# One decode block on one core: heads 28 to 30 selected in two steps, the last head's last two value blocks as matmul weights, and a new order of the last three heads

## The chip, the cores and the metric

The kernel runs on one core of a Trainium2 chip, in float32 throughout. The metric is the device time of one execution in microseconds (us); of several executions the median is taken. "At 358.03" means 358.03 us after the start of the profiled span.

## What is computed

For a batch of 4 with one new token each, a block computes attention over a cache and then a small token-mixing network, both under an adaptive layer norm. Cut to what matters here:

```
q = (h @ wq) as 32 heads of 128;  k, v: 8 cached heads of 4096 x 128 per batch, each serving 4 query heads
p = softmax(q k^T / sqrt(128));   o = p v;   A = o @ wo
x = x + ga * A
h = layernorm(x) * (1 + cb) + sb;   u = gelu(h * w1 + b1) (1792 wide);   y = u . w2 + b2
x = x + gb * y
```

One pair of batch and cached head is called a head below; there are 32 of them, 0 to 31, and heads 24 to 31 belong to the last batch. Each reads 2048 KB of keys and as much of values: 134 of the 157 MB that the kernel loads.

## The kernel before

**Layout.** The scores of a head stand in PSUM as 128 partitions by 1024 columns: four groups of 32 partitions, each a quarter of the keys, made by four matmuls that write to four different groups (`scores`, L238). In each group only 4 of the 32 rows are query heads (a row every 8); the rest are padding. VectorE takes the maximum over a row (L243) and over the groups (L252), ScalarE the exponential with the row sums (L268, tile `p` and `l`), and VectorE transposes `p` in blocks of 32 (`turn`, L275, two halves), so that keys stand on partitions.

**Values of heads 0 to 30** (`values`, L301): 8 matmuls, each with 32 columns of `p` as weights and 512 columns of values moving. A product of 512 columns holds four key blocks of 128 side by side, and of the 128 partitions by 512 columns of the sum `pv` only those places count where a row's key block is that of the column. VectorE copies `pv` to `po` (`copy_v`, L315). The **selection** (`pick`, L324) is 4 matmuls with a 128 x 128 piece of `po` as weights and 4 columns of `sel` moving, summed into `pt` (128 x 4): `sel` holds a 1 at the rows that belong to a query head, times the reciprocal of the sum of exponentials (`sums`, L279; `scale`, L284 and L290). VectorE copies `pt` to `oT` (L329), and `project` multiplies it with `wo` (4 matmuls of 512 columns, L337; VectorE adds the result to `acc`, L353). A float32 matmul is two matmul instructions in the profile, each with a weight load: 4 matmuls appear as x8.

**Head 31** ends in another way (`values_last`, L309): 32 blocks of 128 keys, each one matmul with 32 columns of `p` as weights and 128 columns of values moving; four blocks run in four partition groups. So its sum `pve` is 128 x 128 and its selection one matmul. Heads 30 and 31 project (L342, 16 matmuls of 128 columns each) straight into one PSUM tile, `pgx`, to which a matmul with the identity (L685) adds `ep`, the residual with all earlier heads of the batch (fold L358, then L362 and L363 on VectorE). On `pgx` the layer norm begins (L370), and behind it the whole mixing network of the last batch.

**The order of the work.** From head 24 on it is written out by hand in a string, `PLAN`: each word is a step, its letter an operation, its number the head (and after the dot the part). Those spoken of here: `t` turn, `l` sums, `L` scale, `v` values, `V` copy_v, `a` pick, `A` copy_o, `p` project, `P` add_up, `x` and `g` a piece of the mixing network of batch 2 (VectorE L431, ScalarE L487), `f` a VectorE product of `wo` with a gate (L567), `y` the fold, `E` the residual, `I` the identity matmul, `LV` and `LW` loads. Each engine executes its own share strictly in this order.

**Loads.** All run on one queue, SP's, into a ring of three slots of 4 MB; a load waits only until its slot is free. The values of heads 30 and 31 arrive in pieces, cut at the blocks of `cuts`: (0, 16, 32) and (0, 16, 24, 28, 32). The last load, `LW`, is 1 MB of modulation weights.

**Buffers.** The pool `wk` gives two buffers to a tag unless another number is written; the small PSUM tiles (`pl`, `pm`, `pb`, `pt`, `pa`, `pc`, `pst`) share two buffers of the pool `ps_m`.

Of the kernel before, what the change touches and what calls it, by code (L numbers as in the profile page):

```python
# [8 lines left out]
F32 = mybir.dt.float32  # L9
I32 = mybir.dt.int32  # L10
AF = mybir.ActivationFunctionType
# [22 lines left out]
def adaln_decode(ctx: ExitStack, tc: tile.TileContext, small, x, wmod, wq, kk, kv, vv, wo, out):  # L34
# [53 lines left out]
    first = g32[:, 0:1].to_broadcast([P, 32])  # L88
    QT = cst.tile([P, B, HKV, 32], F32, name="QT")
# [187 lines left out]
    def sums(i):  # L277
        pl = ps_m.tile([P, 1], F32, name="pl", tag="m")
        mm(pl, grp if i < NS - 1 else grpl, PL[i][1], start=True, stop=True)  # L279
        SEL[i] = pl  # L280

    def scale(i):
        rl = wk.tile([P, 1], F32, name="rl")
        dv.reciprocal(rl, SEL[i])  # L284
        if i == NS - 1:
            SEL[i] = wk.tile([P, 1, REP], F32, name="sel", bufs=4)
            dv.tensor_scalar(SEL[i][:, 0], eight, rl, None, op0=OP.mult)
            return
        sel = wk.tile([P, 4, REP], F32, name="sel", bufs=4)
        dv.tensor_scalar(sel, sel4, rl, None, op0=OP.mult)  # L290
        SEL[i] = sel

    PV, PA = {}, {}

# [9 lines left out]
    def values_last(i, ks, pv):  # L304
        PV[i] = pv
        pT = PL[i][0].rearrange("p (k r) -> p k r", r=32)
        for k in ks:
            for c in range(4):
                mm(pv[32 * c:32 * c + 32, :], pT[:, k * 4 + c, :], VT[i][:, k * 4 + c, :],  # L309
                   start=(k == 0), stop=(k == 7))  # L310
# [7 lines left out]

    def pick(i):
        po, sel = PV.pop(i), SEL.pop(i)  # L320
        OT[i] = pt = ps_m.tile([P, REP], F32, name="pt", tag="m")
        n = po.shape[-1] // DH
        for c in range(n):
            mm(pt, po[:, c * DH:(c + 1) * DH], sel[:, c, :], start=(c == 0), stop=(c == n - 1))  # L324

    def copy_o(i):
        pt = OT[i]
        OT[i] = wk.tile([P, REP], F32, name="oT")
        dv.tensor_copy(OT[i], pt)  # L329

    def project(i, pa=None):
        b, h = divmod(i, HKV)
        oT = OT.pop(i)
        if pa is None:
            pa = ps_m.tile([P, D], F32, name="pa", tag="m")
            for g in range(REP):
                mm(pa[32 * g:32 * g + 32, :], oT[:, g:g + 1].to_broadcast([P, 32]), wo_t[h][:, g, :],  # L337
                   start=True, stop=True)
        else:
            for g in range(REP):  # L340
                for c in range(4):
                    mm(pa[32 * c:32 * c + 32, :], oT[:, g:g + 1].to_broadcast([P, 32]),  # L342
                       wo_t[h][:, g, c * P:(c + 1) * P], start=(g == 0 and h == HKV - 2),
                       stop=(g == REP - 1 and h == HKV - 1))
        PA[i] = pa
# [232 lines left out]
    for i in range(NS - HKV):  # L578
# [38 lines left out]
        if i == NS - HKV - 2:  # L617
# [7 lines left out]
    cuts = {NS - 1: (0, 16, 24, 28, 32), NS - 2: (0, 16, 32)}  # L625
    last = [(0, 1, 2, 3), (4, 5), (6,), (7,)]
# [6 lines left out]
    v28.1 b31 l30 B31 e31 LV31 V28 L30 c t30.1 a28 l31 L31 v29.0 t31.1 v29.1 A28 p28 t30.0 V29 a29 v30.0  # L633
    A29 LW f v30.1 P28 p29 g V30 t31.0 a30 x v31.0 v31.1 v31.2 P29 A30 Y y f v31.3 p30 E V31 a31 I A31 p31
# [3 lines left out]
             "l": sums, "L": scale, "V": copy_v, "a": pick, "A": copy_o, "P": add_up,  # L638
# [5 lines left out]
    for step in PLAN.split():  # L644
# [8 lines left out]
        elif op == "v":  # L653
            if i < NS - 1:
                values(i, range(4 * q, 4 * q + 4))
                continue
            if q == 0:
                pve = ps_s.tile([P, 8, P], F32, name="pve", tag="s")[:, 0]
            values_last(i, last[q], pve)
        elif op == "p":  # L660
            project(i, pgx[:, 4] if i >= NS - 2 else None)
# [19 lines left out]
        elif op == "E":  # L681
            ep = cst.tile([P, P], F32, name="ep")
            residual(ep, pc)
        elif op == "I":
# [50 lines left out]
```

## Time and profile before

| what | value |
|---|---|
| time, median of 3 runs | 389.92 us (388.86, 389.92, 390.04) |
| profiled execution: span from first to last instruction | 386.9 us |
| profiled execution: its own time | not listed apart from the three runs, which are 1.9 to 3.1 us above the span |
| TensorE busy, weight loads | 298.9 us, 122.4 us |
| VectorE, ScalarE busy | 215.2 us, 108.0 us |
| loaded from HBM | 157.32 MB, 407 GB/s over the span |
| mean granted TensorE clock | 0.877 of full speed |

In the profile PE is TensorE's matmuls, PEld its weight loads, DVE VectorE, ACT ScalarE and SPq the queue of SyncE, which issues the loads. A row of the timeline has start, duration, engine, line, operation, tiles and shapes; the brackets at its end tell how long the engine had been idle and what released it. The chain of waits is followed back from the last instruction, and its rows are start, duration and what ran or was waited for.

### The profile page before, as it was taken

To read this page: it belongs to the slowest core of one execution; us is meant where nothing else is said; L and a number is where in the kernel's file an instruction comes from. 1 tells how busy PE (TensorE), PEld (TensorE's weight loads), DVE (VectorE), ACT (ScalarE), POOL (GpSimd) and SP (SyncE) were. 2 spreads that over 40 slices of the span, in tenths; PEclk is the share of its full clock that TensorE was granted. 3 is DMA by queue.
4 is the path that set the end of the run, shared out by engine and by line. 5 is a ranking of instruction groups with operands and counts; after the bars stand their busy time and mean duration, and the time that the engine had idled before them with its cause. 6 is when DMAs were issued, how large, how long until landed. Compare 5 with 4: busy or idle time off the path is not lost.

```text
span 386.9 us, 5714 instructions
## 1 busy us (share of the span) xinstructions
PE 298.9 (77%) x2416; PEld 122.4 (32%) x2416; DVE 215.2 (56%) x516; ACT 108.0 (28%) x132; POOL 0.7 (0%) x6
## 2 busy tenths in 40 slices
PE   0765575863966949979888859999988887999984
PEld 0111121231323313334222323443323342444562
DVE  0420351620542524676766644676875579788766
ACT  0101120110110110113567210213783104757356
POOL 0000000000000000000000000000000000000000
PEclk9998875986695775989999985978999998899999
DMA  8999999999999999999999999999999999999910
GB/s 329 430 434 434 415 451 430 410 449 432 418 447 434 430 434 432 434 432 434 426 434 429 434 429 434 434 432 434 425 434 432 434 429 434 422 427 423 404 46 3
DMA packets 7281, 157.70 MB, mean 408 GB/s; under 512 B 964, under 2 KB 980, under 8 KB 1368
## 3 DMA queue, kind: packets, MB, share of 16 engines
q1 hardware_dynamic: 7248, 157.33, 94.8%
q8 instruction: 19, 0.31, 0.3%
q14 instruction: 6, 0.05, 0.0%
q10 hardware_dynamic: 8, 0.00, 0.0%
HBM read 157.32 MB, written 0.01 MB: 407 GB/s over the span
## 4 chain that ended last, share of the span: by engine, by line
DMA 54%; PE 28%; DVE 16%; issue 1%; SPq 1%; ACTq 0%; DVEq 0%
DMA kv<-in_kv 47%; PE s L238 8%; PE pv L301 7%; DMA wq<-in_wq 6%; DVE m L243 3%; DVE p L275 3%; PE pt L324 2%; PE pa L337 2%; PE pb L258 2%; DVE uu L431 1%; DVE mx L252 1%; DVE acc L353 1%; PE qs L152 1%; PE phb L417 1%; PE pve L309 1%
## 5 line engine op out<-in xcount | busy, mean ns | idle before, releaser
L238 PE MATMUL s<-kv,QT 128*32 128x512 f32 x512 | 76.2, 715 | 35.6 <-DMA kv<-in_kv 32.6
L268 ACT ACTIVATE p<-s,nm 128x1024 f32<-128x1024 f32 x32 | 35.6, 1114 | 199.0 <-DVE nm L263 198.9
L243 DVE TENSOR_REDUCE m<-s 128x1 f32<-128x1024 f32 x32 | 39.2, 1224 | 76.1 <-PE s L238 76.0
L301 PE MATMUL pv<-kv,p 128*32 128x512 f32 x496 | 75.0, 684 | 0.4 <-DMA kv<-in_kv 0.4
L275 DVE STREAM_TRANSPOSE p<-p 128x512 f32<-128x512 f32 x64 | 41.9, 687 | 1.7 <-ACT p L268 1.7
L324 PEld LDWEIGHTS pt<-sel,po 128*128 128x128 f32 x250 | 33.6, 208 | 28.7 <-issue 15.6
L238 PEld LDWEIGHTS s<-kv,QT 128*32 128x32 f32 x512 | 16.3, 125 | 81.3 <-DMA kv<-in_kv 45.3
L337 PE MATMUL pa<-wo,oT 128*32 128x512 f32 x240 | 35.3, 663 | 4.3 <-DVE oT L329 4.2
L324 PE MATMUL pt<-sel,po 128*128 128x4 f32 x250 | 36.2, 268 | 1.4 <-DVE po L315 1.4
L315 DVE COPY po<-pv 128x512 f32<-128x512 f32 x31 | 21.4, 689 | 17.0 <-PE pv L301 17.0
L252 DVE TENSOR_REDUCE mx<-pm 1x128 f32<-1x512 f32 x32 | 21.4, 671 | 0.8 <-PE pm L247 0.7
L258 PEld LDWEIGHTS pb<-neg,mx 1*128 1x128 f32 x64 | 10.8, 210 | 32.9 <-DVE mx L252 31.1
L487 ACT ACTIVATE u<-u 128x1024 f32<-128x1024 f32 x20 | 20.4, 1052 | 2.7 <-DVE u L431 2.6
L431 DVE TENSOR_SCALAR u<-hb,wr,sm 128x512 f32<-128x512 f32 x40 | 19.9, 541 | 1.0 <-PE py L442 0.9
L353 DVE TENSOR_TENSOR acc<-acc,pa 128x512 f32<-128x512 f32 x26 | 17.7, 681 | 3.6 <-PE pa L337 3.6
L268 ACT ACT_TABLE_LOAD x11 | 14.1, 1283 | 19.0 <-DVE nm L263 18.9
L137 PE MATMUL s<-wm,sT 128*4 128x512 f32 x16 | 8.4, 684 | 12.2 <-DVE sT L123 12.2
L258 PE MATMUL pb<-neg,mx 1*128 1x1 f32 x64 | 13.5, 278 | 5.3 <-DVE mx L252 5.3
L487 ACT ACT_TABLE_LOAD x13 | 16.7, 1283 | 0.2
L247 PE MATMUL pm<-ident,m 128*1 128x128 f32 x32 | 9.1, 286 | 9.8 <-DVE rl L284 3.8
L301 PEld LDWEIGHTS pv<-kv,p 128*32 128x32 f32 x496 | 14.1, 146 | 8.1 <-issue 2.1
L247 PEld LDWEIGHTS pm<-ident,m 128*1 128x1 f32 x32 | 2.5, 80 | 39.1 <-DVE rl L284 21.0
(144 smaller groups left out, 212.3 us busy)
## 6 DMA issues: line engine op xcount, KB each, us to landing
kv<-in_kv SPq DMA_DIRECT2D x28, 4096.0 KB, 20.8
wq<-in_wq SPq DMA_DIRECT2D x2, 4096.0 KB
wo<-in_wo SPq DMA_DIRECT2D x4, 2048.0 KB
kv<-in_kv SPq DMA_DIRECT2D x4, 2048.0 KB, 18.5
wm<-in_wmod SPq DMA_DIRECT2D x2, 2048.0 KB
kv<-in_kk SPq DMA_DIRECT2D x1, 4096.0 KB
kv<-in_vv SPq DMA_DIRECT2D x3, 1024.0 KB
wm<-in_wmod SPq DMA_DIRECT2D x1, 1024.0 KB
```

The costliest lines, as they stand in the source:

```text
L238: mm(s[32 * c:32 * c + 32, n * 512:(n + 1) * 512], QT[:, b, h, :], KT[i][:, (n * 4 + c) * 512:(n * 4 + c + 1) * 512], start=True, stop=True)
L243: dv.tensor_reduce(M[i], S[i], axis=AX.X, op=OP.max)
L252: dv.tensor_reduce(mx, M[i].rearrange("o (c r) -> o r c", c=4).unsqueeze(1).to_broadcast([1, 4, 32, 4]), axis=AX.X, op=OP.max)
L258: mm(pb, M[i].rearrange("o c r -> o (c r)"), neg1, start=True, stop=True)
L268: nc.scalar.activation(p, S[i], AF.Exp, bias=M.pop(i), accum_out=l)
L275: dv.transpose(p, p)
L301: mm(PV[i][32 * q:32 * q + 32, :], pT[:, 128 * k:128 * k + 128:4], VT[i][:, 4 * k:4 * k + 4, :].rearrange("p j d -> p (j d)"), start=(k < ...
L324: mm(pt, po[:, c * DH:(c + 1) * DH], sel[:, c, :], start=(c == 0), stop=(c == n - 1))
L337: mm(pa[32 * g:32 * g + 32, :], oT[:, g:g + 1].to_broadcast([P, 32]), wo_t[h][:, g, :], start=True, stop=True)
L353: dv.tensor_add(ACC[b], ACC[b], pa)
L431: dv.tensor_scalar(u[:, e, :], hb, wr[:, j:j + 1], b1[:, j:j + 1], op0=OP.mult, op1=OP.add)
L487: nc.scalar.activation(u, u, AF.Gelu_apprx_tanh)
```

## The change

Four things change.

1. **Heads 28, 29 and 30 select in two steps.** `scale` now spreads the reciprocals over 32 columns per key block (`sel32`, 128 x 128 in place of 128 x 16; 28 of 32 columns in a group are zero, from a constant `gsel` built at the start). `gather_heads` multiplies with these as weights and `po` moving: 4 matmuls of 128 columns into four partition groups of a PSUM tile `qo`. `copy_heads` copies `qo` to SBUF, on VectorE for head 28 and on ScalarE for 29 and 30. `pick` is then one matmul, with that copy as weights and 4 columns of a constant moving.
2. **The last head's last two blocks.** `values_last` does blocks 0 to 29. Blocks 30 and 31 (`values_end`) take the values themselves as weights (128 x 128) and 4 columns of `p` moving, straight into `pt`, and the selection of the other 30 blocks is added to the same tile. The scale by the reciprocal moves behind it: `sums` of head 31 makes four sums on all partitions (`le`, `pl4`), `scale` is a reciprocal of 4 columns, and `copy_o` of head 31 multiplies instead of copying.
3. **The cuts of head 31's values** become (0, 16, 24, 30, 32).
4. **A new order of the last lines of `PLAN`,** with head 30's projection in two halves.

```diff
+    gsel = cst.tile([P, 4, 32], F32, name="gsel")
+    dv.memset(gsel, 0.0)
+    dv.tensor_copy(gsel[:, :, 0:REP], sel4)
...
     def sums(i):
+        if i == NS - 1:
+            le = wk.tile([P, REP], F32, name="le", bufs=1)
+            dv.tensor_scalar(le, eight, PL[i][1], None, op0=OP.mult)
+            SEL[i] = ps_m.tile([P, REP], F32, name="pl4", tag="m")
+            mm(SEL[i], ones, le, start=True, stop=True)
+            return
...
     def scale(i):
+        if i == NS - 1:
+            rl4 = wk.tile([P, REP], F32, name="rl4", bufs=1)
+            dv.reciprocal(rl4, SEL[i])
+            SEL[i] = rl4
+            return
         rl = wk.tile([P, 1], F32, name="rl")
         dv.reciprocal(rl, SEL[i])
...
+        src, m = (gsel, 32) if i in TWO else (sel4, REP)
+        sel = wk.tile([P, 4, m], F32, name=f"sel{m}", bufs=4) if m == REP else wk.tile([P, 4, m], F32, name="sel32", tag="h1")
+        dv.tensor_scalar(sel, src, rl, None, op0=OP.mult)
...
+    TWO = (NS - 4, NS - 3, NS - 2)
+    ENDING = 30
...
+    def values_end(i):
+        pT = PL[i][0].rearrange("p (k r) -> p k r", r=32)
+        for j in range(ENDING, 32):
+            mm(OT[i], VT[i][:, j, :], pT[:, j, 0:32:8], start=(j == ENDING), stop=False)
...
+    def gather_heads(i):
+        po, sel = PV.pop(i), SEL.pop(i)
+        QO[i] = q = ps_m.tile([P, P], F32, name="qo", tag="m")
+        for c in range(4):
+            mm(q[32 * c:32 * c + 32, :], sel[:, c, :], po[:, c * DH:(c + 1) * DH], start=True, stop=True)
...
+        QO[i] = wk.tile([P, P], F32, name="qs", tag="a")
+        if i < NS - 3:
+            dv.tensor_copy(QO[i], q)
+        else:
+            nc.scalar.activation(QO[i], q, AF.Copy)
...
     def pick(i):
+        if i in TWO:
+            OT[i] = pt = ps_m.tile([P, REP], F32, name="pt", tag="m")
+            mm(pt, QO.pop(i), g32[:, 0:REP], start=True, stop=True)
+            return
+        if i == NS - 1:
+            mm(OT[i], PV.pop(i), eight, start=False, stop=True)
+            return
...
-        dv.tensor_copy(OT[i], pt)
+        if i == NS - 1:
+            dv.tensor_mul(OT[i], pt, SEL.pop(i))
+        else:
+            dv.tensor_copy(OT[i], pt)
...
-    cuts = {NS - 1: (0, 16, 24, 28, 32), NS - 2: (0, 16, 32)}
-    last = [(0, 1, 2, 3), (4, 5), (6,), (7,)]
+    cuts = {NS - 1: (0, 16, 24, ENDING, 32), NS - 2: (0, 16, 32)}
+    last = [range(8), range(8, 16), range(16, 24), range(24, ENDING)]
...
-    v28.1 b31 l30 B31 e31 LV31 V28 L30 c t30.1 a28 l31 L31 v29.0 t31.1 v29.1 A28 p28 t30.0 V29 a29 v30.0
-    A29 LW f v30.1 P28 p29 g V30 t31.0 a30 x v31.0 v31.1 v31.2 P29 A30 Y y f v31.3 p30 E V31 a31 I A31 p31
+    v28.1 b31 l30 B31 e31 LV31 V28 L30 c j28 J28 t30.1 a28 A28 l31 L31 v29.0 t31.1 v29.1 p28 t30.0 V29 P28
+    j29 J29 v30.0 a29 A29 LW t31.0 f v30.1 p29 g V30 P29 j30 J30 v31.0 a30 v31.1 f A30 Y x y v31.2 v31.3
+    p30.0 E V31 O v31.4 a31 p30.1 I A31 p31
```

Three places show how the change moves instructions. The numbers behind the tiles' names only tell buffers apart; `po_2333` and `po_2336` are head 28's in the two kernels.

TensorE where head 28 is selected and head 31's sums are made, before:

```order
L436 MATMUL py_2065<-u_2135,sm_88 32x128 x8
L324 MATMUL pt_2348<-sel_2255,po_2333 128x4 x4
L279 MATMUL pl_2353<-l_2327,grpl_118 128x1
L301 MATMUL pv_2359<-kv_2210,p_2235 32x512 x8
L337 MATMUL pa_2371<-wo4_126,oT_2369 32x512 x4
```

and in the changed kernel:

```order
L481 MATMUL py_2068<-u_2138,sm_88 32x128 x8
L341 MATMUL qo_2350<-po_2336,sel32_2258 32x128 x4
L357 MATMUL pt_2358<-g32_114,qs_2355 128x4
L285 MATMUL pl4_2364<-le_2362,ones_107 128x4
L313 MATMUL pv_2368<-kv_2213,p_2238 32x512 x8
L382 MATMUL pa_2378<-wo4_129,oT_2360 32x512 x4
```

Between the first and the second step of the selection there is now a copy by VectorE (`qs_2355`), and the sums of head 31 read `le_2362`, which VectorE makes, where before they read `l_2327` from ScalarE. Head 29's values stand behind both.

VectorE at the same place, before:

```order
L315 COPY po_2333<-pv_2295 128x512
L284 RECIPROCAL rl_2335<-pl_2322 128x1
L290 TENSOR_SCALAR sel_2337<-g32_114,rl_2335 128x16
L275 STREAM_TRANSPOSE p_2306<-p_2306 128x512
L284 RECIPROCAL rl_2355<-pl_2353 128x1
L287 TENSOR_SCALAR sel_2357<-g32_114,rl_2355 128x4
L275 STREAM_TRANSPOSE p_2326<-p_2326 128x512
```

and in the changed kernel:

```order
L331 COPY po_2336<-pv_2298 128x512
L297 RECIPROCAL rl_2338<-pl_2325 128x1
L300 TENSOR_SCALAR sel32_2340<-gsel_120,rl_2338 128x128
L347 COPY qs_2355<-qo_2350 128x128
L278 STREAM_TRANSPOSE p_2309<-p_2309 128x512
L374 COPY oT_2360<-pt_2358 128x4
L283 TENSOR_SCALAR le_2362<-g32_114,l_2330 128x4
L293 RECIPROCAL rl4_2366<-pl4_2364 128x4
```

`le_2362` stands behind the copy, a transpose of half of head 30's `p`, and `oT`. The third row, head 30's selection, takes the buffer of head 28's (`sel32_2258`: tag `h1` has two), so it waits until TensorE's four matmuls on `qo_2350` have read that.

TensorE from the values of head 31 to the layer norm, before:

```order
L309 MATMUL pve_2415<-kv_2311,p_2326 32x128 x28
L358 MATMUL pc_2448<-acc_2040,g32_114 32x128 x4
L309 MATMUL pve_2415<-kv_2311,p_2326 32x128 x4
L342 MATMUL pgx_2447<-wo6_127,oT_2445 32x128 x16
L324 MATMUL pt_2479<-sel_2357,po_2477 128x4
L685 MATMUL pgx_2447<-ep_2474,ident_100 128x128
L342 MATMUL pgx_2447<-wo6_127,oT_2482 32x128 x16
```

and in the changed kernel:

```order
L321 MATMUL pve_2427<-kv_2314,p_2329 32x128 x8
L357 MATMUL pt_2436<-g32_114,qs_2425 128x4
L321 MATMUL pve_2427<-kv_2314,p_2329 32x128 x8
L403 MATMUL pc_2452<-acc_2043,g32_114 32x128 x4
L321 MATMUL pve_2427<-kv_2314,p_2329 32x128 x14
L387 MATMUL pgx_2449<-wo6_130,oT_2447 32x128 x8
L326 MATMUL pt_2484<-p_2329,kv_2314 128x4 x2
L360 MATMUL pt_2484<-g32_114,po_2482 128x4
L387 MATMUL pgx_2449<-wo6_130,oT_2447 32x128 x8
L737 MATMUL pgx_2449<-ep_2479,ident_100 128x128
L387 MATMUL pgx_2449<-wo6_130,oT_2497 32x128 x16
```

Head 30's second selection step stands among head 31's values, its first half projection ahead of the last two blocks and its second behind head 31's selection. On ScalarE two copies are new, `qs` of heads 29 and 30, the first ahead of the table load and the gelu of `g`, the second behind them; no table load is added.

41 lines of the change are left out of this document (22 added, 19 removed).

## The prediction

> **What bounds the kernel now.** I read the page first, for the loads, then the chain of waits, then the timeline of the last 30 us engine by engine. From the page, what the loads moved in forty slices of 9.67 us, and the chain's shares:
>
> ```profile
> GB/s 329 430 434 434 415 451 430 410 449 432 418 447 434 430 434 432 434 432 434 426 434 429 434 429 434 434 432 434 425 434 432 434 429 434 422 427 423 404 46 3
> DMA 54%; PE 28%; DVE 16%; issue 1%; SPq 1%; ACTq 0%; DVEq 0%
> ```
>
> The rate stays between 404 and 451 from the second slice to the thirty-eighth, so the loads never pause: their number and size set when the last values arrive, and no engine changes that as long as slots come free early enough. The change loads the same bytes in the same order. A row of the chain says it for the end of the loop, and a row of TensorE's timeline shows what slack the engines have at the start:
>
> ```profile
> 336.33 21.56 DMA kv<-in_kv
> ```
>
> ```profile
> 38.00 3.64 PE L238 MATMUL s<-kv,QT 128*32 128x512 f32 x16 [2.88 <-DMA kv<-in_kk]
> ```
>
> The first is a load that head 29's values wait for; before 358 the engines wait for loads. From there on TensorE is what matters (timelines of PE and PEld, start and duration first):
>
> ```profile
> 357.48 0.36 PE L279 MATMUL pl<-l,grpl 128*128 128x1 f32 x2
> 358.03 1.95 PE L301 MATMUL pv<-kv,p 128*32 128x512 f32 x16 [0.19 <-DMA kv<-in_kv]
> 359.76 1.07 PE L337 MATMUL pa<-wo,oT 128*32 128x512 f32 x8
> 360.79 1.05 PE L324 MATMUL pt<-sel,po 128*128 128x4 f32 x8
> 361.77 2.11 PE L301 MATMUL pv<-kv,p 128*32 128x512 f32 x16
> 362.79 0.21 PEld L301 LDWEIGHTS pv<-kv,p 128*32 128x32 f32 x8 [0.80 <-DMA kv<-in_vv]
> 363.70 1.04 PE L337 MATMUL pa<-wo,oT 128*32 128x512 f32 x8
> 364.70 1.05 PE L324 MATMUL pt<-sel,po 128*128 128x4 f32 x8
> 365.68 1.85 PE L309 MATMUL pve<-kv,p 128*32 128x128 f32 x56
> 367.10 0.16 PEld L309 LDWEIGHTS pve<-kv,p 128*32 128x32 f32 x8 [0.17 <-DMA kv<-in_vv]
> 367.35 0.40 PE L358 MATMUL pc<-acc,g 128*32 128x128 f32 x8
> 367.74 0.16 PEld L309 LDWEIGHTS pve<-kv,p 128*32 128x32 f32 x8 [0.26 <-DMA kv<-in_vv]
> 367.98 1.06 PE L342 MATMUL pgx<-wo,oT 128*32 128x128 f32 x32
> 368.97 0.39 PE L324 MATMUL pt<-sel,po 128*128 128x4 f32 x2
> 369.21 0.47 PE L685 MATMUL pgx<-ep,ident 128*128 128x128 f32 x2
> 369.61 1.08 PE L342 MATMUL pgx<-wo,oT 128*32 128x128 f32 x32
> ```
>
> TensorE issues without a gap, yet meets the loads at 362.79, 367.10 and 367.74, where head 31's blocks 24 to 27 and 28 to 31 land. So the selections of heads 28 to 30 are covered: TensorE made faster there would wait longer at 367.10. What decides is the time from the landing at 367.74 to the start of head 31's projection at 369.61: **1.87 us** = blocks 0.24, projection of head 30 0.99, selection 0.24, identity matmul and wait 0.40. Behind it nothing changes.
>
> **The change, part by part.** Costs are from start to start of neighbouring rows: a selection by 128 x 128 weights 0.98 (360.79 to 361.77) or 0.24 for one matmul (368.97 to 369.21), so 0.12 for each of its two loads; four matmuls of 128 columns in four groups 0.24 (367.74 to 367.98); 16 of them 0.99; four of 512 columns 0.87 (half of 358.03 to 359.76). VectorE's rows, with two of ScalarE behind:
>
> ```profile
> 351.87 0.16 DVE L263 COPY nm<-pb 128x1 f32<-128x1 f32 x1 [0.23 <-PE pb L258]
> 355.82 0.68 DVE L315 COPY po<-pv 128x512 f32<-128x512 f32 x1
> 356.42 0.16 DVE L284 RECIPROCAL rl<-pl 128x1 f32<-128x1 f32 x1
> 356.62 0.24 DVE L290 TENSOR_SCALAR sel<-g,rl 128x16 f32<-128x16 f32 x1
> 356.76 0.71 DVE L275 STREAM_TRANSPOSE p<-p 128x512 f32<-128x512 f32 x1
> 360.04 0.69 DVE L315 COPY po<-pv 128x512 f32<-128x512 f32 x1 [0.45 <-PE pv L301]
> 363.95 0.69 DVE L315 COPY po<-pv 128x512 f32<-128x512 f32 x1 [0.71 <-PE pv L301]
> 367.81 0.29 DVE L362 TENSOR_TENSOR ep<-pc,prep 128x128 f32<-128x128 f32 x1 [0.40 <-PE pc L358]
> 369.39 0.16 DVE L329 COPY oT<-pt 128x4 f32<-128x4 f32 x1 [0.76 <-PE pt L324]
> 10.47 0.22 ACT L119 ACTIVATE sg<-sm 128x16 f32<-128x16 f32 x1
> 374.71 0.69 ACT L425 ACTIVATE hb<-py,mv 128x512 f32<-128x512 f32 x1 [0.92 <-PE py L417]
> ```
>
> *Start.* `gsel` adds a fill and a copy on VectorE, some 0.3 us; the 2.88 us wait for keys at 38.00 hides it. Uncovered it would cost 0.3. The wider `sel32` of heads 28 and 29 adds under 0.1 each, hidden by the wait of 0.23 at 351.87.
>
> *Head 28.* Its copy ends at 356.51, so the four gathering matmuls start at 356.56, as the selection did. A group of 128-column matmuls is seen by VectorE 0.46 after its start (367.35 to 367.81): 357.02. Only then may `sel32` of head 30 be written, whose buffer they read; it and the copy `qs` are two 128 x 128 operations, 0.29 each as L362, overlapped to some 0.5: 357.5. The second matmul runs; VectorE goes on with a transpose (0.62 apart), `oT` and `le` (0.24, as L290) until 358.35. Head 31's sums wait for `le`: 358.4 in place of 357.48, and behind them, 0.3 later, head 29's values: **358.7 in place of 358.03**. Queued behind is every later matmul. The price of no such wait is 0; with both 128 x 128 operations priced as the next larger row (0.69) it is 1.3. I take 0.7, by the rows of the same size.
>
> *Heads 29 and 30, up to head 31.* Values of 29 end their issue at 360.45; `po` starts 2.01 after their start, as before, 360.7, and ends at 361.4; gathering 361.46, head 30's first values 361.7, before 361.77: the shorter selection has already given the delay back. Second step of 29 at 362.6 (ScalarE's copy, 0.22 to 0.69, by its size about 0.35, is done at 362.3), values from 362.85 (landed 362.79), projection 363.7. Now VectorE has a transpose and a gate product (0.6 each) ahead of head 30's `po`: 364.3 in place of 363.95. It ends at 365.0; gathering 365.05, head 31's blocks 0 to 7 at 365.3, second step of 30 after ScalarE's copy at 365.9 to 366.2, blocks 8 to 15, fold, blocks 16 to 23 at 366.2, 366.65, 366.9, done at **367.35**. Blocks 24 to 29 land between 367.10 and 367.74, half way by bytes: **367.42**. TensorE and the loads arrive together.
>
> *From there to the end.* Blocks 24 to 29 are 12 instructions, 0.35. A row pair prices one thing more, the step from 32-column to 128-column weights:
>
> ```profile
> 371.66 0.64 PE L436 MATMUL py<-u,sm 128*32 128x128 f32 x16
> 372.12 0.62 PE L436 MATMUL py<-kv,sm 128*32 128x128 f32 x16
> ```
>
> 16 instructions followed by their like take 0.46, 32 followed by 128-column weights 0.99 and not 0.92: the step costs 0.07. Half of head 30's projection followed by such a step is 0.53, twice. So: blocks 0.35, half projection 0.53, blocks 30 and 31 as weights 0.49 (four loads at 0.12), selection 0.24, half projection 0.53, identity 0.24. Sum **2.38**, from 367.42: head 31's projection starts at **369.80**, before 369.61, **+0.2 us**. Its `oT` (0.4 after the selection's start at 368.8, and 0.16) is ready at 369.4, covered by the second half and the identity; `po` of the 30 blocks, due at 368.8, is ready at 368.3, behind VectorE's two pieces of `x` and `ep`. Uncovered, either would cost up to 0.4. The new shape, values as weights, isn't in the trace: as cheap as 32-column weights (0.03 a load) it saves 0.37, and twice as dear costs 0.49; I take the 128 x 128 loads of L324, the same size.
>
> [...]
>
> **Rivals.** *Faster:* the last blocks decide alone. If TensorE were free when blocks 30 and 31 land at 367.74, the rest would be 0.04 + 0.49 + 0.24 + 0.53 + 0.24 = 1.54: head 31's projection at 369.28, **-0.3 us**, 389.6. For it: 1.87 shrinks to 1.54 behind the last landing. Against it: blocks 24 to 29 and half a projection, 0.88, fit only if the former land by 366.9, and they land at 367.42.
>
> *Slower:* VectorE's queue ahead of `le` and of head 30's `po` makes TensorE late. It decides once blocks 24 to 29 start after 367.42, and my schedule reaches them 0.07 earlier; from there each 0.1 late is 0.1 lost. With the high price above, 0.6 more: **+0.8 us**, 390.7.
>
> *Slower by the clock:*
>
> ```profile
> 326.00:331.00 5.00, 4.78 (x35) 2.70 (x38) 3.30 (x8) 3.46 (x4) 0.00 (x0) 0.50 0.99 426
> 366.00:371.00 5.00, 5.00 (x138) 3.96 (x130) 2.60 (x9) 2.54 (x3) 0.00 (x0) 1.00 0.47 193
> 330.57 2.77 PE L238 MATMUL s<-kv,QT 128*32 128x512 f32 x16
> 340.01 1.92 PE L238 MATMUL s<-kv,QT 128*32 128x512 f32 x16
> ```
>
> The granted clock (the column ahead of the load's share) is 0.50 at 326 and 1.00 at the end; the scores take 2.77 in place of 1.92 while it rises. If it fell over the last 3.4 us of projections, at 1.44 times, **+1.5 us**, 391.4. Against it: the new waits of TensorE are half a microsecond long.
>
> *It doesn't do what it says:* the copies move the bound to another engine. VectorE waits 0.76 and ScalarE idles there, so no.
>
> **How the numbers follow.** The profiled span goes from 386.9 to 387.1; what lies around it (388.86 to 390.04 less 386.9) stays. I carry +0.2 to the median 389.92: **390.1 us**. Chances: forecast, within 0.3 of it, 0.55; faster rival 0.17; slower by VectorE 0.22; clock 0.06. The three runs before lie 1.2 us apart, which widens every case. The bounds of the unknown costs (-0.37, +0.8) and this scatter give **389.2 to 391.0**; outside stay the clock's case and the ends of the scatter. 0.3% is 1.17 us, about what a measurement of this kernel can tell from no change. Beyond it below lies only the faster rival with scatter, 0.06; above it the clock and the end of the slower rival, 0.10; within, 0.84.
>
> **What would show it.** Right: head 29's values about 0.7 later; blocks 24 to 29 with hardly a wait at 367.4; head 31's projection 2.4 behind them. Wrong: a wait of TensorE for the last two blocks (faster rival), or blocks 24 to 29 long after their landing (slower one), or weights of values that cost other than 0.12 a load. The whole forecast falls if the last values land at another time than 367.7, which a pause of the loads or slower short rows (1 KB for the last piece, 2 KB before) could do.

## The result, and the profile after

| kernel | median | range | runs |
|---|---|---|---|
| before | 388.98 us | 388.86 to 390.04 | 9 (the three shown at first and six beside the changed kernel) |
| changed | 391.18 us | 389.66 to 391.54 | 9 |

The ratio over all runs is 1.004 with a 95% interval of 1.0027 to 1.0053 (it is not the quotient of the medians, which is 1.0057). The changed kernel is slower by 0.4%; the interval begins just below the 0.3% that the prediction called no change. The median lies 0.18 us above the end of the predicted range. The nine times stand in two groups: 389.66, 389.80, 389.93, and from 390.70 to 391.54. The profiled execution is the one of 391.54, its span 389.5.

The loads are as before: in the page of the changed kernel the rate stays between 421 and 441 GB/s from the second slice to the thirty-seventh, and the last piece lands at 368.02 (before: 367.70; over all traces of this study 367.67 to 368.05, whichever kernel ran). TensorE's timeline at the places that the prediction spoke of:

```profile
356.27 0.64 PE L481 MATMUL py<-u,sm 128*32 128x128 f32 x16
356.88 0.43 PE L341 MATMUL qo<-po,sel 128*32 128x128 f32 x8
357.91 0.39 PE L357 MATMUL pt<-g,qs 128*128 128x4 f32 x2 [0.61 <-DVE qs L347]
358.80 0.56 PE L285 MATMUL pl<-le,ones 128*128 128x4 f32 x2 [0.51 <-DVE le L283]
359.29 3.35 PE L313 MATMUL pv<-kv,p 128*32 128x512 f32 x16
362.47 1.03 PE L382 MATMUL pa<-wo,oT 128*32 128x512 f32 x8
...
372.09 1.08 PE L387 MATMUL pgx<-wo,oT 128*32 128x128 f32 x32
```

The two new waits are there, 0.61 for head 28's copy `qs` and 0.51 for `le`, and VectorE's rows show the chain that the prediction named ahead of them:

```profile
357.37 0.29 DVE L300 TENSOR_SCALAR sel<-gsel,rl 128x128 f32<-128x128 f32 x1 [0.47 <-PE qo L341]
357.57 0.28 DVE L347 COPY qs<-qo 128x128 f32<-128x128 f32 x1
357.77 0.70 DVE L278 STREAM_TRANSPOSE p<-p 128x512 f32<-128x512 f32 x1
358.40 0.12 DVE L374 COPY oT<-pt 128x4 f32<-128x4 f32 x1
358.44 0.21 DVE L283 TENSOR_SCALAR le<-g,l 128x4 f32<-128x4 f32 x1
```

Then something that the forecast did not have at this place: head 29's values take 3.18 us from start to the next row (359.29 to 362.47), where before they took 1.73 (358.03 to 359.76). The table by windows tells why; its columns after the window's length are the busy times of the engines with their instructions, then the granted clock:

```profile
355.39:358.80 3.41, 2.30 (x34) 1.45 (x31) 2.14 (x9) 1.21 (x2) 0.00 (x0) 1.00 0.96 408
358.80:362.21 3.41, 3.41 (x18) 1.28 (x22) 1.37 (x3) 0.00 (x0) 0.00 (x0) 0.50 1.00 416
```

From 358.80 to 362.21, for 3.41 us, TensorE ran at half its clock. What followed was late by that, and head 31's projection began at 372.09 in place of 369.61. In this trace and in that of the kernel before, every full stretch at one clock is 3.41 us long or a whole multiple of that (up to 119.47 us).

A second profile of the same kernel, from a run of 389.87 us in a later set (below, changed kernel again), had no such fall. Its TensorE rows show the change by itself:

```profile
358.84 0.35 PE L285 MATMUL pl<-le,ones 128*128 128x4 f32 x2 [0.51 <-DVE le L283]
359.13 1.95 PE L313 MATMUL pv<-kv,p 128*32 128x512 f32 x16
360.90 1.04 PE L382 MATMUL pa<-wo,oT 128*32 128x512 f32 x8
...
365.54 0.43 PE L341 MATMUL qo<-po,sel 128*32 128x128 f32 x8 [0.16 <-DVE po L331]
...
368.02 0.30 PE L387 MATMUL pgx<-wo,oT 128*32 128x128 f32 x2
...
368.77 0.61 PE L326 MATMUL pt<-p,kv 128*128 128x4 f32 x4
369.23 0.36 PE L360 MATMUL pt<-g,po 128*128 128x4 f32 x2
369.53 0.64 PE L387 MATMUL pgx<-wo,oT 128*32 128x128 f32 x16
370.10 0.49 PE L737 MATMUL pgx<-ep,ident 128*128 128x128 f32 x2
370.52 0.75 PE L387 MATMUL pgx<-wo,oT 128*32 128x128 f32 x20
```

Head 31's projection starts 2.47 us behind the last landing (370.52 less 368.05) where before it was 1.91 (369.61 less 367.70): **0.56 us lost behind the last landing**, and TensorE waits for no load there any more. The terms are in the rows: the last two blocks 0.46 in place of 0.24, the two halves of head 30's projection 0.75 and 0.57 in place of 0.99 for the whole, the selection 0.30 for 0.24 and the identity matmul 0.42 for 0.40. That is 0.63; 0.07 of it is won back, since the projection starts 0.03 ahead of the last landing, where the kernel before took up its last blocks 0.04 behind it. So two things made the kernel slower: some 0.6 us at the end, and, in the profiled run in which the clock fell, 1.4 us more at head 29's values and 1.6 at head 31's projection.

### The profile page after: what moved, and what is told of

Same layout as the page of the kernel before. It is cut to its first block, busy times and chain, and to the rows that moved or that the text cites. A ratio compares the mean times of both kernels' runs of the same rounds, so it can differ in the third digit from the quotient of the medians.

```text
span 389.5 us, 5732 instructions
## 1 busy us (share of the span) xinstructions
PE 295.5 (76%) x2422; PEld 118.5 (30%) x2422; DVE 215.8 (55%) x519; ACT 108.6 (28%) x134; POOL 0.7 (0%) x6
## 4 chain that ended last, share of the span: by engine, by line
DMA 53%; PE 27%; DVE 16%; ACT 1%; issue 1%; SPq 0%; ACTq 0%; DVEq 0%
DMA kv<-in_kv 52%; PE s L241 6%; PE pv L313 6%; DVE p L278 3%; PE s L140 2%; DVE m L246 2%; PE qs L155 2%; PE pt L366 2%; PE pa L382 2%; DMA sm<-in_small 2%; DVE uu L476 1%; DVE mx L255 1%; DVE acc L398 1%; PE pb L261 1%; DVE wo L612 1%
## 5 line engine op out<-in xcount | busy, mean ns | idle before, releaser
L241 PE MATMUL s<-kv,QT 128*32 128x512 f32 x512 | 73.3, 697 | 42.2 <-DMA kv<-in_kv 40.0
L313 PE MATMUL pv<-kv,p 128*32 128x512 f32 x496 | 73.8, 674 | 1.6 <-DMA kv<-in_kv 1.6
L241 PEld LDWEIGHTS s<-kv,QT 128*32 128x32 f32 x512 | 15.3, 119 | 85.4 <-DMA kv<-in_kv 56.2
L366 PEld LDWEIGHTS pt<-sel,po 128*128 128x128 f32 x224 | 30.7, 212 | 25.5 <-issue 19.2
L366 PE MATMUL pt<-sel,po 128*128 128x4 f32 x224 | 33.0, 271 | 0.8 <-DVE po L331 0.8
L140 PE MATMUL s<-wm,sT 128*4 128x512 f32 x16 | 9.6, 769 | 12.2 <-DVE sT L126 12.2
```

The costliest lines, as they stand in the source:

```text
L241: mm(s[32 * c:32 * c + 32, n * 512:(n + 1) * 512], QT[:, b, h, :], KT[i][:, (n * 4 + c) * 512:(n * 4 + c + 1) * 512], start=True, stop=True)
L313: mm(PV[i][32 * q:32 * q + 32, :], pT[:, 128 * k:128 * k + 128:4], VT[i][:, 4 * k:4 * k + 4, :].rearrange("p j d -> p (j d)"), start=(k < ...
```

## The experiments

Two theories stood at the start. C: the clock falls because of the new waits of TensorE. Q: VectorE's queue ahead of `le` and of head 30's `po` makes TensorE late, and the clock only follows.

Twelve kernels, in four sets; each set ran on one chip and shares its runs of the kernel before. Code is shortened below: of `PLAN` only the words around the change are printed. Since the times of every kernel stand in two groups, the table also counts the **high runs**: those more than 0.7 us above the fastest of the same kernel and set.

| kernel | median | fastest | high runs | ratio to before (interval) |
|---|---|---|---|---|
| before, all sets | 388.98 to 389.74 | 388.64 to 388.86 | 53 of 125 | |
| changed, first set | 391.18 | 389.66 | 6 of 9 | 1.004 (1.0027 to 1.0053) |
| changed kernel again | 390.34 | 389.70 | 6 of 12 | 1.0026 (1.0011 to 1.004) |
| waits filled, 256 columns | 389.84 | 389.35 | 2 of 12 | 1.0014 (1.0 to 1.0028) |
| waits filled, 4 columns | 389.88 | 389.69 | 5 of 12 | 1.0027 (1.0006 to 1.0049) |
| waits and tail filled | 389.84 | 389.67 | 1 of 12 | 1.001 (0.9996 to 1.0024) |
| sums ahead of the copy | 389.78 | 389.52 | 5 of 12 | 1.0011 (0.9993 to 1.0029) |
| two-step selections alone | 389.34 | 388.82 | 5 of 12 | 1.0011 (0.999 to 1.0032) |
| last head alone | 389.43 | 388.96 | 5 of 12 | 1.0013 (0.9992 to 1.0034) |
| before, filled | 389.15 | 388.96 | 2 of 12 | 1.0003 (0.9989 to 1.0018) |
| whole projection (filled) | 389.56 | 389.32 | 3 of 12 | 0.9997 (0.9981 to 1.0013) |
| reordered end (filled) | 389.49 | 389.14 | 1 of 12 | 0.9996 (0.9982 to 1.001) |
| before, split projection | 389.52 | 389.13 | 4 of 12 | 1.0001 (0.9977 to 1.0025) |
| best of both (filled) | 389.08 | 388.83 | 0 of 12 | 0.9987 (0.9973 to 1.0001) |

The medians of before differ by set (388.98, 389.09, 389.09, 389.74, 389.26) mostly by how many of its runs were high: in the set with 389.74 it was 18 of 29.

### The clock, or VectorE's queue

**Both waits of TensorE filled** with matmuls that nobody reads:

```
-  c j28 J28 t30.1 a28 A28 l31 L31 v29.0
+  c j28 J28 D t30.1 a28 A28 D l31 L31 v29.0
+  D: for c in range(4): mm(fill[32*c:32*c+32, 0:256], first, prep[:, 0:256])
```

> The changed kernel with four extra matmuls of 256 columns (about 0.45 us, their result is read by nobody) on TensorE in each of its two new waits: behind the gathering matmuls of head 28, and ahead of head 31's sums. Nothing else moves. Theory C (clock): the two waits, some 1.1 us together, leave TensorE so little to do that the granted clock is halved for one 3.4 us period in most runs, and that is the 1.6 us between the changed kernel's two groups of times (389.7 to 389.9 and 391.2 to 391.5). Then the filled kernel stays in the lower group: median 389.7 to 390.1, none or one of its runs above 391. Theory Q (VectorE's queue alone makes every run late, and where the clock falls is luck): the fill changes nothing, median 390.7 to 391.5 with most runs above 391.

Median 389.84, and no run above 390.75. TensorE's waits are gone but for 0.18, and VectorE's order is that of the changed kernel, but the rows of TensorE differ:

```profile
356.89 0.62 PE L740 MATMUL fill<-prep,g 128*32 128x256 f32 x8
357.68 0.39 PE L357 MATMUL pt<-g,qs 128*128 128x4 f32 x2 [0.18 <-DVE qs L347]
358.00 0.64 PE L740 MATMUL fill<-prep,g 128*32 128x256 f32 x8
```

```profile
353.69:357.10 3.41, 3.41 (x49) 1.63 (x45) 2.51 (x6) 2.34 (x4) 0.00 (x0) 1.00 0.97 413
357.10:360.51 3.41, 3.23 (x36) 1.41 (x32) 2.66 (x8) 0.19 (x2) 0.00 (x0) 1.00 1.00 416
```

The clock stays at 1.00. A kernel that executes 16 matmul instructions more has a median 1.3 us under the changed kernel's first and 0.5 under its second (390.34). The three ran in different sets, and its interval overlaps that of the second, so the medians alone prove little; but 2 of 12 runs are high where the changed kernel has 12 of 21, and the filling leaves VectorE's queue as it was. VectorE's queue alone does not make the high group. So much for the clock; the 0.6 us behind the last landing are still there (head 31's projection at 370.28, 2.52 behind the last landing at 367.76).

**Head 31's sums ahead of the copy**, so that one wait covers both:

```
-  c j28 J28 t30.1 a28 A28 l31 L31 v29.0
+  c j28 l31 J28 t30.1 a28 A28 L31 v29.0
```

> The changed kernel with head 31's sums made ahead of the copy, the transpose and the second step of head 28, on VectorE and on TensorE, so that they no longer stand behind those. TensorE's wait for the copy falls into the sums, and head 29's values start some 0.6 us earlier. Theory C: less idle time and less delay, median 389.2 to 389.7, few runs above 391. Theory Q: 0.6 less in every run but the same two groups, median 390.4 to 390.9.

389.78, a little above what was expected, with its lower times (from 389.52) only 0.1 to 0.2 under the changed kernel's. An earlier start of head 29's values by 0.7 brings nearly nothing. That fits a pace set by the loads: with both waits filled TensorE already reaches blocks 24 to 29 as they land (367.46, landed 367.42). And the profiled run, 391.0, has the clock at half from 358.21 to 361.62 and again from 382.10 to 385.51, so shorter waits alone (one of 0.55 in place of 0.61 and 0.51) did not keep it up.

**Each half of the change alone**, first the two-step selections on the kernel before, then the new ending of the last head:

```
two-step:   -  c t30.1 a28 l31 L31 v29.0 ...   p30 E V31 a31 I A31 p31
            +  c j28 J28 t30.1 a28 l31 L31 v29.0 ...   p30 E V31 a31 I A31 p31
last head:  -  v31.3 p30 E V31 a31 I A31 p31
            +  v31.3 p30 E V31 O v31.4 a31 I A31 p31      (cuts 0, 16, 24, 30, 32; le, rl4)
```

> The kernel before with only the two-step selection of heads 28 to 30; the last head, its cuts and its projection as before. One wait of TensorE, 0.6 us for the copy of head 28, stays; the wait for head 31's sums is gone. Theory C: 0.2 to 0.4 above before in the lower group (389.1 to 389.4) and a minority of runs 1.6 higher. Theory Q: the same 0.2 to 0.4 in every run and no second group beyond that of before.

> The kernel before with only the new ending of the last head: blocks 30 and 31 as weights, the scale behind the selection, the cuts. Head 30's projection stays whole and heads 28 to 30 are selected as before, so TensorE never waits for head 31's sums (the old selection of head 28 covers them). By both theories no second group beyond before's. By the working of the prediction: 30 blocks by 0.35, projection 0.99 and 0.07, weights 0.49, selection 0.24, identity 0.24 behind 367.42 gives 369.8, 0.2 above before: 389.0 to 389.4. If the ending were a gain by itself, 388.5 to 388.8.

389.34 and 389.43, both intervals around 1. The kernel with the two-step selections alone has head 31's projection 1.91 behind the last landing (369.67 less 367.76), exactly as before: the two-step selections neither gain nor lose. The kernel with the last head alone shows something more. In its profiled run of 390.6 the clock fell at 358.45, and there TensorE had **not waited at all**:

```profile
355.04:358.45 3.41, 3.38 (x42) 2.46 (x38) 2.36 (x9) 2.26 (x4) 0.00 (x0) 1.00 0.99 418
358.45:361.87 3.42, 3.42 (x20) 1.08 (x19) 1.28 (x5) 1.34 (x2) 0.00 (x0) 0.50 1.02 423
```

```profile
356.18 0.64 PE L457 MATMUL py<-u,sm 128*32 128x128 f32 x16
356.78 1.05 PE L342 MATMUL pt<-sel,po 128*128 128x4 f32 x8
357.86 0.39 PE L282 MATMUL pl<-le,ones 128*128 128x4 f32 x2
358.25 3.56 PE L307 MATMUL pv<-kv,p 128*32 128x512 f32 x16
```

It was busy for 3.38 of 3.41 us and the clock was halved all the same. So busy time did not keep the clock up there. What is small in that period is the data that passes through the array. I counted for every period of 3.41 us, on the grid that the clock's own changes give, the columns that each matmul record that starts in it streams, times its share of 128 weight columns. In the changed kernel's period from 355.39 it is 24 x 128 x 32/128 = 768 for the rows at 356.27 and 356.88 and 12 for three groups of 1 or 4 columns: **780**. In the period just quoted: 512 for `py`, 32 and 8 for the selection and the sums, 4 for two groups of one column, 512 for the first four records of head 29's values: **1068**. In the kernel before the two periods there hold 2437 and 2210, in the filled one 2053 and 2832. In the second profile of the changed kernel, the one without the fall, the grid stood elsewhere and cut the thin stretch in two, with 1797 and 2576:

```profile
354.43:357.85 3.42, 2.91 (x41) 1.42 (x37) 1.95 (x7) 1.21 (x2) 0.00 (x0) 1.00 1.00 426
357.85:361.26 3.41, 2.80 (x24) 1.38 (x28) 2.33 (x8) 0.00 (x0) 0.00 (x0) 1.00 1.01 420
```

That is how one kernel comes to have two groups of times: the profiled run with the fall took 391.54 us, the one without it 389.87.

Over all fourteen traces I shared out each matmul's columns over its duration, since it can stand across the border of two periods. After the first 23 us, all 121 periods at full clock with under 1350 of this measure were followed by one at half clock, none of the 906 with over 1600, and 10 of the 122 between. Busy time does not part them: of the periods in which TensorE was busy for no more than 2.31 us (2.30 in the changed kernel's from 355.39), the 116 with under 1350 were all followed by half clock and none of the 110 with over 1600 was. So in these traces the fall follows the work and not the waits. That the exact measure of the hardware is this one isn't shown: in the first 23 us, where most matmuls have weights of 4 columns, 22 of 28 low periods were not followed by a fall.

### Work in a period, or idle time

The next set was made to tell these apart. **The changed kernel again**, as the set's base:

> The changed kernel once more, for its times beside the others of this set on one chip. Theory W (work in a window): TensorE's clock halves for 3.41 us after a period of 3.41 us in which few columns were streamed through it; the period is not tied to the kernel's start, so it depends on the run. By counting 128-column matmuls with their share of columns in the earlier trace, low periods can start at 354.8 to 357.6, four fifths of all positions: about two runs in three at 390.5 to 391.6, the others at 389.6 to 389.9. Theory Q (VectorE's queue alone): one group of times around 391.

Six of twelve are high, where two in three were expected: five runs from 389.70 to 389.87, one at 390.23, six from 390.46 to 391.50. One group around 391 is out.

**The waits filled with matmuls of 128 x 128 weights and 4 columns**, which keep TensorE busy and stream next to nothing:

```
+  D: for c in range(3 - q): mm(fill[:, 4*c:4*c+4], ident, g32[:, 0:4])
```

> The changed kernel with TensorE's two waits (ahead of head 28's second step and of head 31's sums) filled with matmuls of 128 x 128 weights that stream 4 columns each: the engine is as busy as in the run with 256-column filling, and streams next to nothing. Theory W: the clock falls as in the changed kernel, median near 391, two thirds of the runs above 390.4. Theory G (the clock falls because TensorE stands idle): as the run with 256-column filling, median 389.8, one run in six above 390.4.

The rows show the waits closed:

```profile
357.23 0.83 PE L740 MATMUL fill<-g,ident 128*128 128x4 f32 x6
357.92 0.38 PE L357 MATMUL pt<-g,qs 128*128 128x4 f32 x2
358.15 0.59 PE L740 MATMUL fill<-g,ident 128*128 128x4 f32 x4
```

Five of twelve runs are high, up to 393.23, nearly as many as in the changed kernel (12 of 21) and more than with 256 columns (2 of 12). That is on the side of the work, but the median, 389.88, is not the 391 that I expected of it; by counts of twelve runs it does not settle the matter by itself. The periods counted above settle it. They also say what this filling should do: if one slides a period of 3.41 us along the kept traces, it holds under 1350 here for 1.15 us of its possible starts in the changed kernel (second profile), for 1.05 with 4-column filling, for 0.80 in the kernel before, and nowhere with 256 columns.

**Filling also in the tail**, where TensorE waits for the last head's gelu. The same count finds a second low place there, for periods that start between 375.9 and 377.3, which the kernel before has too (374.9 to 376.3):

```
+  finish: mm(tail[32*c:32*c+32, 0:n], first, prep[:, 0:n]) for four c,
+          n = 512 ahead of the first block, 128 ahead of the pairs
```

> The changed kernel with 256-column filling in the two waits at 357 to 358.8, and more filling where TensorE waits for the last head's gelu after 376 (four matmuls of 512 columns ahead of the first, four of 128 ahead of the next ones), inside waits of 1.02 and 0.30 to 0.52. Theory W: the second low stretch, 375 to 378, which the kernel before has too, is gone as well: all runs at 389.5 to 390.0, none above 390.4. If the remaining high runs have another cause: one in six above 390.4, as without the filling in the tail.

Eleven of twelve runs from 389.67 to 390.07 and one at 390.54: of the runs that should all have lain between 389.5 and 390.0, two do not, and one of them is high. **The kernel before with such filling:**

```
-  c t30.1 a28 l31 L31 v29.0
+  c t30.1 a28 D l31 L31 v29.0     (four matmuls of 384 columns, and the tail)
```

> The kernel before with four matmuls of 384 columns between head 28's selection and head 31's sums, and the same filling of the tail. Head 29's values start 0.65 later; the wait of 0.80 for loads at 362.79 takes that up, so nothing is lost. Theory W: the high runs of the kernel before (about a quarter, at 390 to 391.7) go: all runs at 388.7 to 389.4, median 388.9. Theory G: TensorE has no gap there, so the high runs stay as frequent as in the kernel before; median 389.1.

Ten of twelve from 388.96 to 389.37, two at 390.76 and 390.96. High runs are fewer than in the kernel before, not gone, and the lowest times are 0.3 above the kernel before's. Five kernels with both places filled (the tail, and the stretch ahead of head 29's values; three follow below) have 7 high runs in 60; the changed kernel had 12 in 21, and the kernel before 53 in 125. A high run that is left need not come from these two places: the one profiled below (whole projection) has half clock from 309.05 to 312.46 and from 329.53 to 336.35.

### The price behind the last landing

From the landing of blocks 24 to 29 to head 31's projection the prediction had summed 2.38; the profile without the fall has 2.79 (367.73 to 370.52). Two suspects: the steps between 32-column and 128-column weights, of which the change adds two, and VectorE's lateness with head 30's copy `po`.

**Head 30's projection whole again**, ahead of the last two blocks, in the filled kernel:

```
-  p30.0 E V31 O v31.4 a31 p30.1 I A31 p31
+  p30.0 p30.1 E V31 O v31.4 a31 I A31 p31
```

> The changed kernel with all the filling, and head 30's projection whole, ahead of the last two value blocks, where the changed kernel has half of it between head 31's selection and the identity matmul. That is two steps less between 32-column and 128-column weights. Theory M (each such step costs about 0.1 us, in both directions): from the landing of blocks 24 to 29 to the start of head 31's projection 2.6 in place of 2.8 to 2.9; head 31's projection at 370.1 in place of 370.3 to 370.4; 389.6 in place of 389.84. Theory N (the steps are free, and the 0.4 missing from my sum is something else): 2.8 or more, since the wait for oT, 0.64 behind the selection, is no longer covered by half a projection; 389.9.

Its profiled run is the high one just named, 1.6 us late already at head 28's selection, so only durations are read from it:

```profile
369.63 1.12 PE L387 MATMUL pgx<-wo,oT 128*32 128x128 f32 x30
370.68 0.61 PE L326 MATMUL pt<-p,kv 128*128 128x4 f32 x4
371.14 0.36 PE L360 MATMUL pt<-g,po 128*128 128x4 f32 x2
371.37 0.47 PE L748 MATMUL pgx<-ep,ident 128*128 128x128 f32 x2
371.77 0.43 PE L387 MATMUL pgx<-wo,oT 128*32 128x128 f32 x8
```

From the first projection record (369.50) to head 31's projection it takes 2.27; in the changed kernel, from 368.02 to 370.52, 2.50. Two steps less, **0.23 less**. The median, 389.56, is what theory M expected. The reverse, **the kernel before with its projection split**, the same instructions and two steps more:

```
-  v31.3 p30 E V31 a31 I A31 p31
+  v31.3 p30.0 E V31 a31 p30.1 I A31 p31
```

> The kernel before with head 30's projection in two halves around head 31's selection, nothing else: the same instructions, with two more steps between 32-column and 128-column weights. Theory M: head 31's projection 0.3 later, 369.9 in place of 369.61, since VectorE's copy po, ready at 368.63, lets the selection start earlier only by 0.3 and both new steps lie behind it; 389.3 where no clock falls. Theory N: 0.0 to 0.1 later, 389.0 to 389.1.

```profile
368.17 0.62 PE L342 MATMUL pgx<-wo,oT 128*32 128x128 f32 x16
368.87 0.39 PE L324 MATMUL pt<-sel,po 128*128 128x4 f32 x2
369.19 0.64 PE L342 MATMUL pgx<-wo,oT 128*32 128x128 f32 x16
369.76 0.49 PE L687 MATMUL pgx<-ep,ident 128*128 128x128 f32 x2
370.18 1.08 PE L342 MATMUL pgx<-wo,oT 128*32 128x128 f32 x32
```

Head 31's projection is 2.30 behind the last landing (370.18 less 367.88), 0.39 more than before; some 0.15 of it is a wait for VectorE's `po`, which ends at 368.82, and the rest is two steps. In both directions a step costs about a tenth of a microsecond: the next weight load starts 0.18 to 0.20 behind the start of the last matmul, where groups of one kind follow each other at 0.11. Since the instructions are the same, the order, and with it the steps, is what costs.

**VectorE's transpose out of the way of `po`**, and half of the projection ahead of blocks 24 to 29:

```
-  j29 J29 v30.0 a29 A29 LW t31.0 f v30.1 ...   v31.2 v31.3 p30.0 p30.1 E V31
+  j29 J29 t31.0 v30.0 a29 A29 LW f v30.1 ...   v31.2 p30.0 v31.3 p30.1 E V31
```

> As the kernel with the whole projection, and head 31's first transposes on VectorE ahead of head 29's oT, so that head 30's copy po is no longer behind them, and head 30's projection in halves, ahead of blocks 24 to 29 and behind them. Theory P (TensorE's lateness by VectorE's queue is made up of that transpose): head 30's po at 364.1 in place of 364.56, its gathering at 364.9 in place of 365.3, head 31's projection at 369.5 to 369.6 in place of 370.3 to 370.4: 389.0, a tie with the kernel before, or 0.1 under it. If VectorE's queue doesn't matter here: no earlier than with the whole projection alone, 389.6.

Theory P falls. `po` moves by 0.1, not by 0.45 (by 0.2, if one allows for the loads, which end 0.12 later in this run), because VectorE now waits for TensorE:

```profile
364.45 0.69 DVE L331 COPY po<-pv 128x512 f32<-128x512 f32 x1 [0.29 <-PE pv L313]
```

Head 31's projection starts at 369.95, not at 369.5. It is 2.07 behind the last landing (367.88), better than the changed kernel's 2.47 by the two steps and by work done ahead of the landing. This transpose in VectorE's queue was not the price here: head 30's values end late on TensorE itself.

**The best of both**: the kernel before with two-step selections, the filling, the transpose early, and a quarter of head 30's projection in TensorE's wait for the last four blocks. The ending of the last head by values as weights is left out.

```
-  ... a29 A29 LW f v30.1 P28 p29 g V30 j30 J30 t31.0 x v31.0 ...  Y y f v31.3 p30 E V31 a31 I A31 p31
+  ... t31.0 v30.0 a29 A29 LW f v30.1 P28 p29 g V30 j30 J30 x v31.0 ...  Y y f p30.0 v31.3 p30.1 E V31 a31 I A31 p31
```

> The kernel before with the two-step selections alone, and three things that the runs so far point to: the filling (four matmuls of 256 columns in the wait for head 28's second step, and in the tail); head 31's first transpose on VectorE ahead of head 29's oT, in its wait there; a quarter of head 30's projection ahead of the last four value blocks, in TensorE's wait for them. No step between 32-column and 128-column weights is added behind the last landing. Theories W and M: head 31's projection at 369.45 to 369.5 in place of 369.61 before and 369.67 with the two-step selections alone; where no clock falls 388.8 to 388.9; at most 2 of 12 runs above 390, median 388.9, under the kernel before's on the same chip (389.1 to 389.7 by how many of its runs are high). If TensorE's wait for the last blocks isn't free for the quarter: head 31's projection at 369.7, median 389.1.

```profile
367.89 0.40 PE L374 MATMUL pgx<-wo,oT 128*32 128x128 f32 x8
368.11 0.40 PE L314 MATMUL pve<-kv,p 128*32 128x128 f32 x8
368.32 0.84 PE L374 MATMUL pgx<-wo,oT 128*32 128x128 f32 x24
...
369.74 1.08 PE L374 MATMUL pgx<-wo,oT 128*32 128x128 f32 x32
```

All twelve runs lie between 388.83 and 389.18. Its median, 389.08, is under the kernel before's 389.26 on that chip, but the interval of the ratio, 0.9973 to 1.0001, just takes in 1. Head 31's projection is 1.72 behind the last landing (369.74 less 368.02) where before it was 1.91: the 0.2 are there, while in this run the loads themselves ended 0.3 later, so the start that I had expected, 369.45 to 369.5, was missed. Nor do the fastest runs show the 0.2: 388.83 here, 388.82 in the kernel before. What the version shows is that none of its twelve runs is high, where beside it 8 of 17 runs of the kernel before were.

## Why the prediction was wrong, and where it was right

The median, 391.18, lies outside the range. The lower group, 389.66 to 389.93, lies inside it and close to the forecast of 390.1, but that is luck: the carry began some 1.1 too high (389.92, where the lower group of the kernel before begins at 388.86), and the sum behind the landing was 0.4 too low. Two steps failed: the chance of the clock's case, and the price of the steps of TensorE behind the landing of blocks 24 to 29.

- **Loads that never pause, and the last landing unchanged:** right. The last landing, at 368.05 in the changed kernel's profile without the fall, is 0.35 later than before, but the same spread is found among runs of all kernels.
- **Head 28 and `le`:** the mechanism and the size were right. The chain of VectorE took from the start of the gathering to the end of `le` 1.77 (356.88 to 358.65); the prediction had 1.79 (356.56 to 358.35).
- **The delay given back, and TensorE and the loads arriving together:** right within 0.1. In the filled kernel blocks 24 to 29 are loaded at 367.46, 0.04 behind their landing at 367.42.
- **From there to the end: the step that failed among the terms of the sum.** I had 0.35, 0.53, 0.49, 0.24, 0.53, 0.24; measured were 0.29, 0.75, 0.46, 0.30, 0.57, 0.42. The values as weights cost what I took (0.46, four loads at 0.12). Wrong were the first half projection, 0.75, and the identity matmul, 0.42. I priced the step from 32 to 128 columns at 0.07 and only in that direction; it is 0.09 there and 0.07 to 0.09 on the way back. For the identity I took 0.24 and put the other 0.16 of the kernel before's 0.40 down to the wait for `oT`, though most of that gap is matmul and step, and stays when `oT` is early (369.79 against 370.52 in the profile without the fall). The rest of the first half projection, 0.2, is not a step: the whole projection behind the same blocks takes 1.18 (369.50 to 370.68), where the kernel before's takes 0.99 with the same step at its end, and where all four groups are full ahead of it, in the best of both, 24 instructions take 0.77. I put it down to the blocks 28 and 29, which fill only two of the four groups; no run changes that alone. So +0.2 should have been +0.6.
- **The rival *slower by the clock*: the step that decided the median.** Its price, 1.5, came out (1.4 on head 29's values, 1.6 at head 31's projection), though at another place than the one it was worked out for. Its chance, 0.06, was wrong, and so was the reason given: "the new waits of TensorE are half a microsecond long". The length of a wait isn't what counted (with the last head alone the clock fell with none), and even the kernel before had 53 high runs in 125. The waits stand among small matmuls that stream little, 780 in the whole period where the kernel before had over 2200, and one period of 3.41 us like that was enough. I also looked for the fall in the last projections only, where the matmuls are dense. The price rests on a length of 3.4 us: the kernel before was at 0.50 for 3.41 us from 49.02 and for twice that from 325.50. Where the periods stand differs from run to run: one begins at 355.39 in the changed kernel's first profile, at 354.43 in its second, at 355.04 with the last head alone.
- **The rival *slower by VectorE's queue*:** the size, +0.8, is about what the low group lost, but not by this mechanism. With `po` no longer behind the transpose, TensorE was hardly earlier.
- **The rival *faster*:** did not come. The last blocks were not what TensorE waited for, as the prediction had argued.
- **The median before.** I carried a difference to a median of three runs of which two were high (389.92, 390.04). The lowest times, 388.86 before and 389.66 after, differ by 0.80, and the rest of the distance between the medians is the share of high runs.

## What to carry to other kernels

Where a run's time comes in two groups, find what separates them before pricing a change: a change that thins out the matmuls over a few microseconds can move runs from one group to the other, which here cost more (1.6 us at head 31's projection) than the change itself (0.6). Ahead of dense matmuls, look for 3.4 us, the length of a period in these traces, in which TensorE streams few columns (here under 1350, each counted with its share of 128 weight columns), waits or not, and give it work there that nobody needs; that left 7 of 60 runs high over five kernels, where the changed kernel had 12 of 21, and in the best of them twelve of twelve runs agree within 0.35 us. And count the steps between 32-column and 128-column weights, 0.07 to 0.09 us each here, in both directions, when a tail is cut into smaller pieces.

## What the runs showed of the hardware

- The granted clock fell after a period in which TensorE was busy 3.38 of 3.41 us, about half of it with 128 x 128 weights and 1 to 4 moving columns. Over fourteen traces and behind the first 23 us, all 121 periods at full clock that streamed under 1350 columns (times the share of 128 weight columns) were followed by half clock, and none of the 906 over 1600.
- A fall of 3.41 us over matmuls of 512 columns costs 1.4 us (3.18 against 1.77 for head 29's 16 instructions).
- A step between 32-column and 128-column weights costs 0.07 to 0.09 us in either direction, read from the distance of the next weight load to the last matmul, 0.18 to 0.20 against 0.11.
- The last landing differs by 0.4 us (367.67 to 368.05) between runs whose loads are the same, so an effect of that size at the end is read from the distance to the landing, not from the start of the span.
